# Even groups across batch borders, two shared PSUM banks for small products, a table that sets the order, and the first batch's keys turned on TensorE

## The chip, the cores and the metric

The kernel runs on one core of one Trainium2 chip. The metric is the device time of one execution in microseconds; the number reported is the median over the executions. A core has five engines, each of which runs its own instructions strictly in its own order and waits on the others through semaphores: TensorE (matrix products and the loading of their weights), VectorE, ScalarE, GpSimd, and SyncE, whose queue only issues DMA transfers here. Products land in PSUM, eight banks of 2 KB per partition.

## The reference

Agent attention is followed by a maxout feed-forward network of three branches. There are B = 4 batches of N = 12544 tokens with C = 128 channels, 49 agents per batch, and a hidden width of 768:

```python
scale = 1.0 / np.sqrt(q.shape[-1])
def sm(a, b):
    s = scale * (a @ b.transpose(0, 2, 1))
    s = s - s.max(-1, keepdims=True)
    e = np.exp(s)
    return e / (e.sum(-1, keepdims=True) + 1e-09)
agent_v = sm(agents, k) @ v          # agents look at all keys of their batch
x = sm(q, agents) @ agent_v          # each token looks at the 49 agents
h = np.maximum(np.maximum(x @ w1, x @ w2), x @ w3)
out = h @ w_out                      # 50176 x 128, float32
```

The inputs q, k, v and the result are 25.7 MB each in float32. All keys and values of a batch must be seen before the first token of that batch can be finished.

## The kernel before

**Tiles and groups.** A batch is 98 tiles of 128 tokens. Tiles go in groups of eight (GT = 8), so a batch has 12 full groups and one of two tiles: 13 groups, 52 in all (NG = 13). Each group exists twice, as a key group (`k_group`) and as a query group (`q_group`).

**Key group.** k and v are loaded (512 KB each), cast to bf16 on GpSimd (for batch 0 the v cast is on ScalarE), and k is turned by a DMA transpose (L159). TensorE makes the scores of 49 agents for each tile (L166), ScalarE the exponentials (`e_k`, L171), TensorE the weighted sums of v and the sums of the exponentials (`values`, L178 and L180, 16 small products), and VectorE adds them to `Eacc` (L189).

**Tail of a batch's keys.** `k_tail` divides (L208 to L211) and multiplies the result by the combined weights `wall`, in four products of 512 or 256 columns (L220) whose copies alternate between ScalarE (L225) and VectorE (L223). This gives G, the 49 x 1792 matrix with which a query's exponentials are turned straight into hidden units. The weights are stored as differences (w2 - w1, w3 - w1), so that the maximum of three becomes relu, add, maximum, and what is left is linear in x.

**Query group.** Eight tiles are loaded, cast and turned by DMA (L253). The scores with the agents (L259) go through the exponential on ScalarE (`e_q`, L264). For each of six hidden chunks f there is a first pair of products into a tile of two PSUM banks (`uv_ps`, L287, called u below), a relu on ScalarE into `a_sb` (L301), a second pair (v, L287) and the maximum with `a_sb` on VectorE into r (L312). For the last chunk, f = 5, ScalarE applies relu in place (L298), the second pair adds on top, and ScalarE's relu (L310) writes r5. The two products of a pair use partitions 0-48 and 64-112. The output comes in two halves o = 0, 1 of four tiles: two linear products (L317), then 24 products with `wo_bf` (L326), and a scale by `recips` on VectorE (L333). The row sums for `recips` come from four tiny products (L273), which share a PSUM tile with the key scores of the same moment, and a reciprocal (L279). One store (L340) writes the group.

**PSUM.** `uv` has three tiles of two banks; "o" (an output half) has one bank, and "m" (scores, sums, key values, k_tail's products) has one.

**Order.** Each step is recorded with a number by `at(key, fn)`; at the end all steps are sorted by it and issued in that order, so the numbers set the order on every engine, SyncE's queue too. One query group takes 6 units. Loads stand 24 units ahead, casts 14, transposes 8 to 10. The keys of batch b run beside the queries of batch b - 1, a group ahead, so the last batch's queries run with no keys beside them, and batch 0's keys run alone at the start.

## Time and profile before

| what | us |
|---|---|
| median of 3 runs | 605.72 (605.44 to 606.43) |
| the profiled execution | 602.93 |
| its span, first to last instruction | 601.1 |
| TensorE busy | 471.4 (78%) |
| VectorE busy | 383.8 (64%) |
| ScalarE busy | 412.5 (69%) |
| GpSimd busy | 140.3 (23%) |

Busy times come from the first part of the profile's page. Matrix products overlap and their ends are modelled in the profile, so TensorE's share is no share of its peak. An instruction's row names its line in the kernel, the engine, the operation, the output and inputs by tile name, shapes and a count; the idle time of the engine just before stands in brackets with what ended it. The mean granted clock of TensorE is 0.948 of full speed.

### The profile page before, as it was taken

To read this page: it belongs to the slowest core of one execution; us is meant where nothing else is said; L and a number is where in the kernel's file an instruction comes from. 1 tells how busy PE (TensorE), PEld (TensorE's weight loads), DVE (VectorE), ACT (ScalarE), POOL (GpSimd) and SP (SyncE) were. 2 spreads that over 40 slices of the span, in tenths; PEclk is the share of its full clock that TensorE was granted. 3 is DMA by queue.
4 is the path that set the end of the run, shared out by engine and by line. 5 is a ranking of instruction groups with operands and counts; after the bars stand their busy time and mean duration, and the time that the engine had idled before them with its cause. 6 is when DMAs were issued, how large, how long until landed. Compare 5 with 4: busy or idle time off the path is not lost.

```text
span 601.1 us, 13157 instructions
## 1 busy us (share of the span) xinstructions
PE 471.4 (78%) x5320; PEld 285.2 (47%) x5320; DVE 383.8 (64%) x499; ACT 412.5 (69%) x493; POOL 140.3 (23%) x149
## 2 busy tenths in 40 slices
PE   0343588898987889888887878889896898889886
PEld 0333245555553545555553545555553444545454
DVE  1200267878786556878776568787875667766774
ACT  2542378787875667787875678878784577777773
POOL 1223543233142232323142232322000101010000
PEclk9999999999998969999997989999996889988999
DMA  8999999999898797989986899995732625533222
GB/s 325 370 340 343 341 275 303 270 294 219 252 239 225 222 277 198 270 269 202 255 261 196 216 284 224 284 257 159 181 110 53 189 77 147 145 119 101 67 75 81
DMA packets 135112, 130.99 MB, mean 218 GB/s; under 512 B 107079, under 2 KB 110091, under 8 KB 135051
## 3 DMA queue, kind: packets, MB, share of 16 engines
q1 hardware_dynamic: 133632, 128.48, 76.7%
q10 hardware_dynamic: 1419, 1.67, 0.8%
q8 instruction: 41, 0.67, 0.5%
q14 instruction: 20, 0.16, 0.1%
HBM read 78.74 MB, written 25.69 MB: 174 GB/s over the span
## 4 chain that ended last, share of the span: by engine, by line
PE 49%; ACT 18%; DVE 15%; DMA 9%; issue 6%; SPq 1%; POOL 1%; ACTq 0%; POOLq 0%; DVEq 0%
PE uv_ps L287 20%; PE o_ps L326 18%; ACT a_sb L301 14%; DVE r L312 12%; DMA kT<-k_bf 6%; PE o_ps L317 4%; PE m_ps L259 3%; DVE o_sb L333 3%; ACT r L310 2%; DMA qT<-q_bf 1%; PE m_ps L178 1%; PE m_ps L180 1%; DMA wst<-in_moe_w_dram 1%; PE m_ps L220 1%; POOL k_bf L150 1%
## 5 line engine op out<-in xcount | busy, mean ns | idle before, releaser
L312 DVE TENSOR_TENSOR r<-uv_ps,a_sb 128x1024 bf16<-128x1024 f32 (+1 forms) x260 | 295.0, 1158 | 40.7 <-ACT a_sb L301 27.7
L301 ACT ACTIVATE a_sb<-uv_ps 128x1024 bf16<-128x1024 f32 (+1 forms) x260 | 248.3, 975 | 71.7 <-PE uv_ps L287 69.9
L287 PE MATMUL uv_ps<-e_q,G 49*128 49x512 bf16 (+1 forms) x1248 | 211.8, 391 | 55.0 <-ACT a_sb L301 43.6
L326 PE MATMUL o_ps<-wo_bf,r 128*128 128x128 bf16 x2352 | 184.1, 227 | 0.0
L326 PEld LDWEIGHTS <-r 128*128 128x128 bf16 x2352 | 144.4, 101 | 52.0 <-issue 49.2
L287 PEld LDWEIGHTS <-G 49*128 49x128 bf16 x1248 | 65.5, 95 | 131.8 <-issue 93.4
L333 DVE TENSOR_TENSOR o_sb<-o_ps,recips 128x512 f32<-128x512 f32 (+1 forms) x100 | 67.0, 670 | 95.1 <-PE o_ps L326 95.1
L249 POOL CAST q_bf<-q_st 128x1024 bf16<-128x1024 f32 (+1 forms) x52 | 51.7, 994 | 154.3 <-DMA qT<-q_bf 150.0
L155 POOL CAST v_bf<-v_st 128x1024 bf16<-128x1024 f32 (+1 forms) x39 | 38.7, 993 | 207.4 <-PE m_ps L180 187.2
L298 ACT ACTIVATE uv_ps<-uv_ps 128x1024 f32<-128x1024 f32 (+1 forms) x52 | 49.9, 959 | 28.5 <-DVE r L312 16.0
L310 ACT ACTIVATE r<-uv_ps 128x1024 bf16<-128x1024 f32 (+1 forms) x52 | 50.7, 975 | 21.5 <-PE uv_ps L287 21.4
L150 POOL CAST k_bf<-k_st 128x1024 bf16<-128x1024 f32 (+1 forms) x52 | 51.9, 998 | 55.5 <-DMA kT<-k_bf 46.4
L317 PE MATMUL o_ps<-G,e_q 128*128 128x256 bf16 x196 | 40.3, 287 | 12.7 <-DVE o_sb L333 12.5
L166 PE MATMUL m_ps<-agT,kT 128*128 128x49 bf16 x392 | 20.9, 196 | 25.7 <-DMA kT<-k_bf 24.4
L178 PE MATMUL m_ps<-e_k,v_bf 128*128 128x49 bf16 x392 | 30.8, 195 | 8.7 <-ACT e_k L171 8.7
L171 ACT ACTIVATE e_k<-m_ps 128x392 bf16<-128x392 f32 (+1 forms) x52 | 25.0, 480 | 16.1 <-PE m_ps L166 15.8
L189 DVE TENSOR_TENSOR Eacc<-m_ps,Eacc 128x98 f32<-128x98 f32 x48 | 10.6, 221 | 35.7 <-PE m_ps L180 35.7
L264 ACT ACTIVATE e_q<-m_ps 128x512 bf16<-128x512 f32 (+1 forms) x52 | 29.5, 568 | 3.7 <-PE m_ps L259 3.6
L317 PEld LDWEIGHTS <-e_q 128*128 128x128 bf16 x196 | 15.0, 98 | 35.1 <-issue 34.5
L180 PE MATMUL m_ps<-e_k,ones 128*128 128x49 bf16 x392 | 30.9, 194 | 0.0
L180 PEld LDWEIGHTS <-ones 128*128 128x128 bf16 x392 | 26.0, 103 | 10.0 <-issue 10.0
L166 PEld LDWEIGHTS <-kT 128*128 128x128 bf16 x392 | 17.3, 104 | 28.3 <-DMA kT<-k_bf 25.7
(43 smaller groups left out, 137.3 us busy)
## 6 DMA issues: line engine op xcount, KB each, us to landing
k_st<-in_k_dram SPq DMA_DIRECT2D x48, 512.0 KB, 5.4
v_st<-in_v_dram SPq DMA_DIRECT2D x48, 512.0 KB, 6.2
q_st<-in_q_dram SPq DMA_DIRECT2D x48, 512.0 KB, 4.2
out_dram<-o_sb SPq DMA_DIRECT2D x48, 512.0 KB, 2.9
wst<-in_moe_w_dram ACTq DMA_DIRECT2D x3, 384.0 KB, 7.8
kT<-k_bf SPq DMA_TRANSPOSE x52, 5.2
qT<-q_bf SPq DMA_TRANSPOSE x52, 4.5
k_st<-in_k_dram SPq DMA_DIRECT2D x4, 128.0 KB, 4.6
```

The costliest lines, as they stand in the source:

```text
L150: nc.gpsimd.tensor_copy(out=d["kb"][:, :n, :], in_=d["k"][:, :n, :])
L155: nc.gpsimd.tensor_copy(out=d["vb"][:, :n, :], in_=d["v"][:, :n, :])
L180: nc.tensor.matmul(t[:, c + A:c + 2 * A], ones, e, start=False, stop=True, skip_group_check=True)
L249: nc.gpsimd.tensor_copy(out=d["qb"][:, :n, :], in_=d["q"][:, :n, :])
L287: nc.tensor.matmul(t[:, h, :T], G[b][h * H:h * H + A, col + f * P:col + (f + 1) * P], d["e"][h * H:h * H + A, :T], start=start, stop=True, ...
L298: nc.scalar.activation(u, u, AF.Relu)
L301: nc.scalar.activation(a_sb[f][:, :, :T], u, AF.Relu)
L310: nc.scalar.activation(r[:, :, :T], u, AF.Relu)
L312: nc.vector.tensor_tensor(out=r[:, :, :T], in0=u, in1=a_sb[f][:, :, :T], op=ALU.max)
L317: nc.tensor.matmul(t[:, i * 2 * C:(i + 1) * 2 * C], d["e"][:, jj * P:(jj + 1) * P], G[b][:, C1O:C1O + 2 * C], start=(i == 0), stop=False, ...
L326: nc.tensor.matmul(t[:, c:c + C], r_sb[f][:, h, jj * P:(jj + 1) * P], wo_bf[:, f, :], start=False, stop=(f == NF - 1), skip_group_check=True)
L333: nc.vector.tensor_tensor(out=d["out"][:, j:j + m, :], in0=d["o", o][:, :m * C].rearrange("p (j c) -> p j c", c=C), in1=d["r"][:, j:j + m] ...
```

## The change

The two files differ in five ways.

1. **Even groups.** The tiles of all batches are one row of 392, cut into 49 groups of eight. Three query groups and the key groups at the borders hold tiles of two batches (`split`); their scores, hidden products, loads and stores are issued in one piece per batch. Batch 0's keys keep 12 groups and one of two tiles, and one key group of six tiles completes the cut.
2. **Small PSUM tiles.** "o" and "m" become one pool of two banks ("om"), which output halves, scores, sums and key products take in turn. k_tail's products (now two, of 1024 and 768 columns, one copied by ScalarE and one by VectorE), and the weight preparation, take `uv` tiles.
3. **Order.** A table `KEY` gives every step of a group its own number. Output products are issued per hidden chunk (`oc01`: half 0, chunk 1), four at a time.
4. **First batch's keys.** They are turned by eight TensorE transposes into a `uv` tile and a VectorE copy (`evacuate`) in place of the DMA transpose.
5. **Buffers.** Loads get four buffers in place of three, the casts of k and q three in place of two, that of v four.

On VectorE, in a regular group with keys beside it, before and after (r0 to r5 are the maxima of hidden chunks, `recips` the reciprocal, `o_sb` an output half's scale, `Eacc` the keys' accumulation):

```order
L312 TENSOR_TENSOR r1_4444<-uv_ps_4428,a_sb_4417 128x1024
L312 TENSOR_TENSOR r2_4484<-uv_ps_4450,a_sb_4446 128x1024
L279 RECIPROCAL recips_4486<-m_ps_4419 128x8
L189 TENSOR_TENSOR Eacc_2820<-m_ps_4419,Eacc_2820 128x98
L333 TENSOR_TENSOR o_sb_4491<-o_ps_4403,recips_4315 128x512
L312 TENSOR_TENSOR r3_4499<-uv_ps_4493,a_sb_4488 128x1024
L312 TENSOR_TENSOR r4_4535<-uv_ps_4505,a_sb_4501 128x1024
L333 TENSOR_TENSOR o_sb_4491<-o_ps_4517,recips_4315 128x512
L312 TENSOR_TENSOR r0_4586<-uv_ps_4561,a_sb_4559 128x1024
```

```order
L371 TENSOR_TENSOR r0_4449<-uv_ps_4437,a_sb_4431 128x1024
L371 TENSOR_TENSOR r1_4484<-uv_ps_4472,a_sb_4440 128x1024
L340 RECIPROCAL recips_4492<-m_ps_4451 128x8
L392 TENSOR_TENSOR o_sb_4519<-o_ps_4397,recips_4321 128x512
L224 TENSOR_TENSOR Eacc_2760<-m_ps_4451,Eacc_2760 128x98
L371 TENSOR_TENSOR r2_4534<-uv_ps_4516,a_sb_4460 128x1024
L371 TENSOR_TENSOR r3_4575<-uv_ps_4544,a_sb_4490 128x1024
L371 TENSOR_TENSOR r4_4595<-uv_ps_4549,a_sb_4498 128x1024
L392 TENSOR_TENSOR o_sb_4519<-o_ps_4531,recips_4321 128x512
L371 TENSOR_TENSOR r0_4620<-uv_ps_4608,a_sb_4602 128x1024
```

The reciprocal and the accumulation stood behind r2, now the reciprocal stands behind r1, and the scale of the first output half between it and the accumulation.

On TensorE, around the key values of such a group, before and after (`v_bf` and `ones` are the weights of the key values, `uv_ps` the hidden products, `m_ps` scores, `o_ps` an output half):

```order
L326 MATMUL o_ps_6412<-wo_bf_91,r5_6399 128x128
L178 LDWEIGHTS v_bf_6012
L178 MATMUL m_ps_6428<-e_k_6451,v_bf_6012 128x49
...
L180 MATMUL m_ps_6428<-e_k_6451,ones_72 128x49
L287 LDWEIGHTS G_4820
L287 MATMUL uv_ps_6502<-e_q_6380,G_4820 128x512
...
L287 MATMUL uv_ps_6505<-e_q_6380,G_4820 128x512
...
L287 MATMUL uv_ps_6514<-e_q_6380,G_4820 128x512
...
L287 MATMUL uv_ps_6523<-e_q_6380,G_4820 128x512
...
L317 MATMUL o_ps_6526<-G_4820,e_q_6209 128x256
...
L259 MATMUL m_ps_6529<-qT_6290,agT_74 64x512
```

```order
L385 MATMUL o_ps_4397<-wo_bf_91,r4_4424 128x128
L214 LDWEIGHTS v_bf_4069
L214 MATMUL m_ps_4451<-e_k_4470,v_bf_4069 128x49
...
L217 MATMUL m_ps_4451<-e_k_4470,ones_72 128x49
L346 LDWEIGHTS G_2826
L346 MATMUL uv_ps_4516<-e_q_4391,G_2826 128x512
...
L346 MATMUL uv_ps_4522<-e_q_4391,G_2826 128x512
...
L319 MATMUL m_ps_4527<-qT_4311,agT_74 64x512
...
L376 MATMUL o_ps_4531<-G_2826,e_q_4219 128x256
```

Four hidden pairs followed the key values, and the linear products stood ahead of the next query scores; now two hidden pairs follow, then the query scores, then the linear products of the second half.

In SyncE's queue, where the first query group's transpose is issued, before and after:

```order
L159 DMA_TRANSPOSE kT_576<-k_bf_538 128x2x128
L245 DMA q_st_582<-in_q_dram 128x1024
L144 DMA k_st_584<-in_k_dram 128x1024
L144 DMA v_st_586<-in_v_dram 128x1024
L159 DMA_TRANSPOSE kT_616<-k_bf_578 128x8x128
L245 DMA q_st_624<-in_q_dram 128x1024
L144 DMA k_st_626<-in_k_dram 128x1024
L144 DMA v_st_628<-in_v_dram 128x1024
L253 DMA_TRANSPOSE qT_635<-q_bf_618 128x8x128
```

```order
L167 DMA k_st_624<-in_k_dram 128x768
L167 DMA v_st_626<-in_v_dram 128x768
L305 DMA q_st_661<-in_q_dram 128x1024
L167 DMA k_st_667<-in_k_dram 128x1024
L167 DMA v_st_669<-in_v_dram 128x1024
L305 DMA q_st_700<-in_q_dram 128x1024
L167 DMA k_st_706<-in_k_dram 128x1024
L167 DMA v_st_708<-in_v_dram 128x1024
L188 DMA_TRANSPOSE kT_734<-k_bf_702 128x6x128
L305 DMA q_st_736<-in_q_dram 128x1024
L167 DMA k_st_742<-in_k_dram 128x1024
L167 DMA v_st_744<-in_v_dram 128x1024
L313 DMA_TRANSPOSE qT_746<-q_bf_732 128x8x128
```

Before, transposes of keys stand between the loads; now the batch's key loads are all issued, and the first DMA transpose is that of the six-tile key group, ahead of the first query transpose.

The diff, without what only follows from the new index names:

```diff
+    NK = -(-NT // GT)
+    NQ = B * NT // GT
...
+    KEY = {
+        "s": -0.90, "ex": -0.41, "u0": 0.94, "u1": 0.95, "a0": 1.77, "v0": 2.04, "a1": 2.06,
...
-    def uv_tile():
-        return psum.tile([P, 2, 512], FP32, tag="uv", bufs=3, name="uv_ps")
-
-    def o_tile():
-        return psum.tile([P, 512], FP32, tag="o", bufs=1, name="o_ps")
-
-    def m_tile(dtype=FP32):
-        return psum.tile([P, 512 if dtype == FP32 else 1024], dtype, tag="m", bufs=1, name="m_ps")
+    def uv_tile(dtype=FP32):
+        return psum.tile([P, 2, 512 if dtype == FP32 else 1024], dtype, tag="uv", bufs=3, name="uv_ps")
+
+    def small_tile(name, dtype=FP32):
+        return psum.tile([P, 512 if dtype == FP32 else 1024], dtype, tag="om", bufs=2, name=name)
...
+
+    def prep_linear():
+        t = uv_tile(BF16)
...
+    def split(t0, t1, step):
+
+        parts = []
+        for t in range(t0, t1, step):
+            i = (t - t0) // step
+            if parts and parts[-1][0] == t // NT:
+                parts[-1][2] = i + 1
+            else:
+                parts.append([t // NT, i, i + 1])
+        return parts
...
         def transposes():
             d["kT"] = work.tile([P, GT, P], BF16, tag="kT", bufs=3, name="kT")
-            nc.sync.dma_start_transpose(out=d["kT"][:, :n, :],
-                                        in_=d["kb"][:, :n, :].rearrange("p j c -> p (j c)"))
+            if early:
+                t = d["kT_ps"] = uv_tile(BF16)
+                for j in range(n):
+                    nc.tensor.transpose(t[:, 0, j * P:(j + 1) * P], d["kb"][:, j, :], ident)
+            else:
+                nc.sync.dma_start_transpose(out=d["kT"][:, :n, :],
+                                            in_=d["kb"][:, :n, :].rearrange("p j c -> p (j c)"))
+
+        def evacuate():
+            nc.vector.tensor_copy(out=d["kT"][:, :n, :].rearrange("p j c -> p (j c)"),
+                                  in_=d["kT_ps"][:, 0, :n * P])
...
+        cols = {b: 0 if i else GT * A for i, (b, _, _) in enumerate(parts)}
+
         def values():
             t = d["s"]
-            c = GT * A
-            for j in range(n):
+            for j in reversed(range(n)):
                 e = d["e"][:, j * A:(j + 1) * A]
-                nc.tensor.matmul(t[:, c:c + A], d["vb"][:, j, :], e, start=False, stop=True,
+                c = cols[batch[j]]
+                nc.tensor.matmul(t[:, c:c + A], d["vb"][:, j, :], e,
+                                 start=(len(parts) > 1 and j == n - 1), stop=True,
...
+        if early:
+            at(key - 24, load)
+            at(key - 5, cast)
+            at(key, transposes)
+            at(key + 0.5, evacuate)
+            at(key + 6.6, scores)
+            at(key + 7, exps)
+            at(key + 13.2, values)
+            at(key + 13.6, accumulate)
+        else:
+            at(key - 22, load)
+            at(key - 11, cast)
+            at(key - 6.5, transposes)
+            at(key + KEY["ks"], scores)
+            at(key + KEY["ke"], exps)
+            at(key + KEY["kv"], values)
+            at(key + KEY["ka"], accumulate)
...
-        def product(i):
-            c0, c1 = i * 512, min((i + 1) * 512, WC)
-            t = m_tile()
-            for h in range(2):
-
-                c = c0 + (C if c0 >= C1O and h == 0 else 0)
...
+        def product(c0, c1, on_vector):
+            t = uv_tile()
+            cuts = [c for c in range(c0, c1, 512)] + [c1]
+            for i, (a, z) in enumerate(zip(cuts, cuts[1:])):
+                for lo, hi in ((a, min(z, C1O)), (max(a, C1O), z)):
...
+                        c = lo + (C if lo >= C1O and h == 0 else 0)
+                        nc.tensor.matmul(t[h * H:(h + 1) * H, i, lo - a:hi - a], d["avT"],
+                                         wall[:, c:c + hi - lo], start=True, stop=True,
+                                         skip_group_check=True)
+            src = t.rearrange("p i c -> p (i c)")[:, :c1 - c0]
+            if on_vector:
+                nc.vector.tensor_copy(out=G[b][:, c0:c1], in_=src)
+            else:
+                nc.scalar.activation(G[b][:, c0:c1], src, AF.Copy)
 
         at(key, normalise)
-        for i in range(-(-WC // 512)):
-            at(key + 0.02 * (i + 1), lambda i=i: product(i))
...
         def hidden(f, col, start):
-            if start:
-                t = uv_tile()
-            else:
-                t = uv[f]
-            for h in range(2):
-                nc.tensor.matmul(t[:, h, :T], G[b][h * H:h * H + A, col + f * P:col + (f + 1) * P],
-                                 d["e"][h * H:h * H + A, :T], start=start, stop=True,
-                                 skip_group_check=True)
+            t = uv_tile() if start else uv[f]
+            for b, j0, j1 in parts:
+                for h in range(2):
+                    nc.tensor.matmul(t[:, h, j0 * P:j1 * P],
+                                     G[b][h * H:h * H + A, col + f * P:col + (f + 1) * P],
+                                     d["e"][h * H:h * H + A, j0 * P:j1 * P], start=start and j0 == 0,
+                                     stop=True, skip_group_check=True)
             return t
...
-        def out_hidden(o, part):
+        def out_hidden(o, f):
             t = d["o", o]
-            for i, h, f in part:
-                jj = pairs[o][i]
-                c = (i * 2 + h) * C
-                nc.tensor.matmul(t[:, c:c + C], r_sb[f][:, h, jj * P:(jj + 1) * P], wo_bf[:, f, :],
-                                 start=False, stop=(f == NF - 1), skip_group_check=True)
+            for i, jj in enumerate(pairs[o]):
+                for h in range(2):
+                    c = (i * 2 + h) * C
+                    nc.tensor.matmul(t[:, c:c + C], r_sb[f][:, h, jj * P:(jj + 1) * P], wo_bf[:, f, :],
+                                     start=False, stop=True, skip_group_check=True)
...
+        cut = 6.0 * (s + 1) + KEY["u0"] - 0.2 if s + 1 in tails else 1e9
         at(key - 24, load)
-        at(key - 14, cast)
-        at(key - 10.2, transposes)
+        at(key - 13, cast)
+        at(key - 9, transposes)
+        at(key + KEY["s"], scores)
+        at(key + KEY["ex"], exps)
+        at(key + KEY["sum"], sums)
+        at(key + KEY["rec"], recips)
         for f in range(NF):
-            at(key + f - 0.95, lambda f=f: first(f))
-            at(key + f - 0.4, lambda f=f: relu_first(f))
-            at(key + f, lambda f=f: second(f))
-            at(key + f + 0.5, lambda f=f: max_second(f))
-        e = key + 6
...
-            at(e + linear, lambda o=o: out_linear(o))
-            for i in range(parts):
-                part = whole[i * per:(i + 1) * per]
-                at(e + first_step + i, lambda o=o, part=part: out_hidden(o, part))
-            at(e + scaled, lambda o=o: out_scale(o))
+            for name, fn in (("u", first), ("a", relu_first), ("v", second), ("x", max_second)):
+                at(min(key + KEY[f"{name}{f}"], cut), lambda f=f, fn=fn: fn(f))
+        for o in range(2):
+            at(key + KEY[f"lin{o}"], lambda o=o: out_linear(o))
+            for f in range(NF):
+                at(key + KEY[f"oc{o}{f}"], lambda o=o, f=f: out_hidden(o, f))
+            at(key + KEY[f"sc{o}"], lambda o=o: out_scale(o))
+        at(key + KEY["sc1"] + 1.5, store)
...
+    first_key = -6.0 * (NK + 2) - 4
+    at(first_key - 30, prep)
+    at(first_key + 24, prep_weights)
+    at(first_key + 36, prep_linear)
+    for g in range(NK):
+        k_group(g * GT, min((g + 1) * GT, NT), first_key + 6.0 * g, True)
+    k_tail(0, first_key + 6.0 * NK + 8)
+    if NT % GT:
+        k_group(NT, NK * GT, -6.0, False)
+    for i in range(NK, NQ):
+        k_group(i * GT, (i + 1) * GT, 6.0 * (i - NK), False)
+    tails = {b * NT // GT: b for b in range(1, B)}
+    for s, b in tails.items():
+        k_tail(b, 6.0 * s + KEY["u0"] - 0.15)
+    for s in range(NQ):
+        q_group(s)
```

163 lines of the change are left out of this document (71 added, 92 removed), and 7 rows, old and new, of the table KEY.

## The prediction

> **What bounds the kernel now.** I read the busy time by stage first, then single regular groups, then the order on the engines. The columns of a window are its length, busy time and count for TensorE, its weight loads, VectorE, ScalarE and GpSimd, the granted clock, the DMA share and GB/s:
>
> ```profile
> 0.00:72.00 72.00, 23.28 (x348) 17.38 (x350) 10.83 (x34) 24.52 (x34) 23.23 (x29) 1.00 1.07 345
> 72.00:450.14 378.14, 323.25 (x3790) 197.31 (x3786) 272.04 (x341) 286.54 (x341) 106.23 (x110) 0.95 0.89 238
> ```
>
> The first 72 us hold no output work: TensorE is busy for 23 of them. Then two regular groups, one with the key stage of the next batch beside it, one after all keys are done:
>
> ```profile
> 257.55:267.29 9.74, 8.48 (x108) 5.37 (x108) 7.54 (x9) 7.88 (x10) 3.01 (x3) 1.00 0.88 262
> 498.33:507.76 9.43, 8.23 (x84) 4.64 (x82) 7.21 (x9) 7.44 (x9) 1.16 (x2) 1.00 0.48 141
> ```
>
> A group takes 9.74 us with keys and 9.43 us without. ScalarE fills 7.88 and 7.44 of them, VectorE 7.54 and 7.21, and DMA moves 262 GB/s. So no engine but TensorE (8.48 and 8.23) is near full, and the profile models the ends of its products. The chain that ended last says the same:
>
> ```profile
> PE 49%; ACT 18%; DVE 15%; DMA 9%; issue 6%; SPq 1%; POOL 1%; ACTq 0%; POOLq 0%; DVEq 0%
> ```
>
> TensorE's order, broken by two waits per group, sets the period. Here are its bursts in that group (start, duration, count, idle before):
>
> ```profile
> 257.55 0.61 PE L287 MATMUL uv_ps<-e_q,G 49*128 49x512 bf16 x4
> 258.40 0.38 PE L317 MATMUL o_ps<-G,e_q 128*128 128x256 bf16 x2 [0.24 <-DVE o_sb L333]
> 258.62 0.61 PE L326 MATMUL o_ps<-wo_bf,r 128*128 128x128 bf16 x8
> 259.06 0.36 PE L166 MATMUL m_ps<-agT,kT 128*128 128x49 bf16 x8
> 259.36 0.61 PE L287 MATMUL uv_ps<-e_q,G 49*128 49x512 bf16 x4
> 259.90 0.62 PE L326 MATMUL o_ps<-wo_bf,r 128*128 128x128 bf16 x8
> 260.45 0.39 PE L287 MATMUL uv_ps<-e_q,G 49*128 49x512 bf16 x2
> 260.77 0.25 PE L273 MATMUL m_ps<-sel,e_q 128*128 128x2 bf16 x4
> 261.14 0.39 PE L287 MATMUL uv_ps<-e_q,G 49*128 49x512 bf16 x2
> ...
> 261.92 0.19 PE L178 MATMUL m_ps<-e_k,v_bf 128*128 128x49 bf16 x1
> ...
> 262.43 0.82 PE L287 MATMUL uv_ps<-e_q,G 49*128 49x512 bf16 x6
> 264.15 0.39 PE L287 MATMUL uv_ps<-e_q,G 49*128 49x512 bf16 x2 [0.90 <-ACT a_sb L301]
> ```
>
> I take a burst's price from start to next start. Hidden products (L287) run in pairs: four cost 0.54, two 0.32, six about 0.76, and of each about 0.1 is the turn to another kind of product. Eight output products (L326) cost 0.44, or 0.55 when a hidden burst follows; two linear ones (L317) 0.22; key scores 0.30, key values 0.51, sums 0.37; query scores, also two of 512 columns, I take as 0.33. At 257.55 four hidden products should leave 0.85 after 0.43 but wait for the single "o" bank, and at 262.43 six are followed only after 1.72 instead of 0.65. These two waits are 0.42 + 1.07 = 1.49 us; without them the sequence is 9.74 - 1.49 = 8.25.
>
> **The regular group after the change.** The new order has 6 hidden bursts per group (4, 2, 2, 6, 4, 6) where 7 stood, and the same products. Its bursts in order, at the prices above: 0.54 (u0, u1), 0.77 (outputs x12), 0.32 (v0), 0.33 (outputs x4), 0.32 (u2), 0.30 (key scores), 0.22 (x4), 0.37 (sums), 0.76 (v1, u3, u4), 0.45 (x8), 0.51 (key values), 0.54 (v2, u5), 0.33 (query scores), 0.77 (linear, x8), 0.76 (v3, v5, v4), 0.44 (x8), 0.55 (linear, x4) = 8.28 us. So the work for TensorE stays; what can be won is the 1.49 of waits, if the new order has fewer. For that I lay ScalarE and VectorE beside it:
>
> ```profile
> 247.95 1.93 ACT L301 ACTIVATE a_sb<-uv_ps 128x1024 bf16<-128x1024 f32 x2
> ...
> 255.81 0.59 ACT L264 ACTIVATE e_q<-m_ps 128x512 bf16<-128x512 f32 x1
> ```
>
> ```profile
> 252.80 0.21 DVE L279 RECIPROCAL recips<-m_ps 128x8 f32<-128x8 f32 x1 [0.16 <-PE m_ps L180]
> ...
> 253.05 0.68 DVE L333 TENSOR_TENSOR o_sb<-o_ps,recips 128x512 f32<-128x512 f32 x1
> 253.65 2.35 DVE L312 TENSOR_TENSOR r<-uv_ps,a_sb 128x1024 bf16<-128x1024 f32 x2
> ```
>
> ScalarE starts a second relu 0.91 after a first, with the result at 1.02; e_q takes 0.59. VectorE starts a second maximum 1.13 after a first (2.35 for two, result at 1.2), reciprocal and accumulation follow at 0.12 each, and out_scale holds it for 0.60. A burst of two is ready for its reader 0.43 after its start (the 0.39 of the row and a hand-over of 0.04). With u0 at 0: relu a0 0.43-1.45, a1 to 2.36, a2 2.39-3.41, e_k to 3.8, a3 3.82-4.84, a4 to 5.75. VectorE finishes the last group's scale at 1.88, r0 at 2.99, and v1 stands at 3.17, so r1 runs 3.60-4.80. Here is the one wait I find: the recips row now stands behind r1, and the key values on TensorE wait for recips, since they share one tile. At 0.06 per hand-over that lets the values start at 5.1 and not at 4.4. Behind them in TensorE's queue stand v2, u5, the next query scores and the second output half; all shift by 0.7. Then v2 at 5.6, u5 ready at 6.25, its relu to 7.25, query scores at 6.15 (their bank was freed by out_scale at 5.6), v3, v5, v4 from 7.25 (the second of them needs the relu at 7.25 and comes at 7.47), e_q to 7.75, r5 7.9-8.9, and the next u0, which needs r5's bank, at 9.0. So **9.0 us with keys**: 8.28 plus 0.7. Without keys neither scores nor values nor that wait are there (8.28 - 0.70 = 7.58); u3, u4, u5 and the query scores then wait 0.1 to 0.3 each for relus and scale, and the layout closes at **8.1**. Bounds: from below 8.3 and 7.6 (no wait at all), from above 9.74 and 9.43 (every old wait finds a new place). I take the layout's, since each of its steps has a row.
>
> The second small bank costs nothing: it takes the "o" wait of 0.42 away and is the same space as before. In the K stage DMA must carry 2.6 MB per group (three loads, one store of 0.52, two transposes of 0.26), 290 GB/s at 9.0 us; the start ran at 345 with a share of 1.07, so I count no wait, and see the rivals.
>
> **Borders.** The same relu (of a regular place in the order) around the three borders, start and duration in us:
>
> ```profile
> 177.14 1.03 ACT a_sb L301
> ...
> 311.74 1.03 ACT a_sb L301
> ...
> 443.48 1.03 ACT a_sb L301
> ...
> 488.90 1.03 ACT a_sb L301
> ```
>
> Twelve full groups and a small one lie between the first two: 134.60 - 12 x 9.74 = 17.7 for a border with its small group. The next is 131.74 - 116.9 = 14.9, the last (three groups at 9.43) 45.42 - 28.3 = 17.1. Together 49.7 us. The new kernel has 49 even groups in place of 52, so the small ones (2 of 8 tiles, at nearly half a group's instructions) are gone, and the tail that builds G is two products and two copies in a row of three 2-bank tiles instead of four, each waiting for the single bank:
>
> ```profile
> 185.71 0.18 PE L180 MATMUL m_ps<-e_k,ones 128*128 128x49 bf16 x1
> 187.17 0.41 PE L220 MATMUL m_ps<-wall,avT 128*64 128x512 bf16 x2 [1.27 <-DVE avT L211]
> 188.26 0.41 PE L220 MATMUL m_ps<-wall,avT 128*64 128x512 bf16 x2 [0.69 <-ACT G L225]
> ...
> 190.90 1.46 PE L287 MATMUL uv_ps<-e_q,G 49*128 49x512 bf16 x6
> ```
>
> The normalise chain is 1.3 and each product step 1.1-1.2. New: normalise stands behind r3 and r4 on VectorE (done at 9.9 in the layout), takes 0.75, first product 0.65, copy 1.0 on ScalarE; then u0, due at 9.0, starts at 12.4: 3.4 late. A group of two batches has its hidden products cut in two, 12 more pairs at about 0.05: 0.6. And the clock falls here:
>
> ```profile
> 189.00:192.00 3.00, 1.86 (x10) 0.67 (x10) 1.40 (x4) 0.62 (x2) 1.04 (x1) 0.65 1.03 393
> 192.00:195.00 3.00, 2.31 (x15) 0.98 (x13) 2.29 (x3) 2.19 (x3) 0.00 (x0) 0.50 0.22 87
> ```
>
> At half clock TensorE's bursts take longer; two windows of 3 us passed below full clock. I add 2 us, and take **6 per border, 18 in all** (bounds 4, with the clock up, and 9, twice such a fall). The clock staying up gives 516 - 6 = 510, and I hold it for 0.1 of the chances, inside the forecast's 0.55. The Trainium skill, "TensorE: Matmul & The Clock Gate", section "HAM oscillation", asks for no idle gap over about 3.4 us. By that rule gaps of 1.7 and 1.1 us would leave the clock alone, which is the 510. The trace disagrees: gaps of 1.27 and 0.69 ended in 0.65 and 0.50.
>
> **The start.** Of 13 early groups, keys are turned by eight transposes and a copy from a uv bank in place of a DMA transpose. Two pure-load stretches and the weights' queue:
>
> ```profile
> 5.00:8.00 3.00, 0.35 (x4) 0.21 (x4) 1.50 (x5) 1.06 (x1) 0.77 (x1) 1.00 1.01 401
> 8.00:12.00 4.00, 0.00 (x0) 0.00 (x0) 0.00 (x0) 0.25 (x1) 1.04 (x1) 1.00 1.04 402
> ```
>
> ```profile
> q10 hardware_dynamic: 1419, 1.67, 0.8%
> ```
>
> The keys and values of a batch are 12.85 MB and the weights 1.67: 14.5 MB at 402 GB/s is 36 us, from 2 us on: 38, where the loads before took turns with 13 transposes. Cast (1.0), turn and copy (1.7), scores, exps, values (2), an estimate from like operations of the same sizes, end at about 44. But q's first DMA transpose stands in SP's queue behind the loads of three more key groups and three q groups, 5.5 MB or 14 us. Before it took this long to land, and the first relu of the first and of the third group ran here:
>
> ```profile
> 61.99 8.09 DMA qT<-q_bf
> ...
> 72.09 1.03 ACT a_sb L301
> ```
>
> ```profile
> 93.78 1.03 ACT a_sb L301
> ```
>
> Landing was 8.09 after issue, and 2 us later the first relu ran. Now issue at about 45.5 plus 8.1, or 38 + 14 + 1: both give 53-54, and the first relu at **56** in place of 72.1. Bounds: 49, if q is ready when G is; 72, if the start is bound by something the trace does not show. Casts (ScalarE 1.06 + 0.50 per group) fit in the 2.8 us that a group's load takes. The Trainium skill, "DMA: Bandwidth & Descriptors", section "Where 436 GB/s comes from", gives about 358 GB/s for a core's loads from HBM; by it they end 4 us later (sum 520, inside the forecast). The rows of 401 and 402 disagree.
>
> **The end.** In the last group r4 is done 8.6 after the first relu, then come 0.22 of products, scale 0.7, the second half's products 1.7, scale 0.7, and the store:
>
> ```profile
> out_dram<-o_sb SPq DMA_DIRECT2D x48, 512.0 KB, 2.9
> ```
>
> With 2.9 for landing, about 14.5 from the first relu of the last group.
>
> **Sum.** 56 + 2.2 (the first two groups took 93.78 - 72.09 = 21.7 in place of 2 x 9.74) + 36 x 9.0 = 324 + 18 + 12 x 8.1 = 97.2 + 14.5 = 511.9 us of span. The profiled execution took 602.93 for a span of 601.1, 1.83 more, and the median of the runs shown is 605.72, 2.79 above that. So 511.9 + 4.6 = **516 us**.
>
> **Rivals.** (1) The order wins nothing in a regular group, because each wait only moves; start and borders are still won. For it: every hidden product still waits for one of three 2-bank tiles. Against it: the old 0.90 wait came from two tiles asked for in a row, which the new order spreads. 516 + 36 x 0.73 + 12 x 1.33 = 558. (2) No wait at values, and q early: 8.4 and 7.9, start 49: 516 - 21.6 - 2.4 - 7 = 485. For it: VectorE has 1.5 us to spare per group. (3) DMA decides in the 36 groups with keys: transposes come late since 290 GB/s with stores is more than the 262 of a regular group. Were it held to 262, a group takes 10.0: 516 + 36 = 552. Against it: 345-402 in the start. (4) Slower: one small bank carries key scores, e_k, recips, values, accumulation, then an output half until its scale, and only then the next key scores. The bare steps are 0.5 + 0.5 + 0.2 + 0.6 + 0.2 + 0.2 + 1.5 + 0.7 = 4.4 us. If each of its three steps on VectorE sits behind two maxima (2 x 1.2 x 3 = 7.2), the loop is 11.6 and 49 groups take 49 x 2.6 = 127 more: 644. It decides above 9.0 and makes the kernel slower above 10.8 (605.7 - 516 over 49 groups). Against it: in VectorE's new order at most one maximum stands right ahead of each.
>
> **Chances.** Forecast 0.55 (its own range 498-534: +-0.3 per group, the start 50-60, borders 4-9), (1) 0.15, (2) 0.16, (3) 0.10, (4) 0.03, no difference 0.01. Leaving out most of (4) and the ends of (1) and (2), 8 in 10 lie in 484-556. Changes under 0.2%, 1.2 us, cannot be told from none here: faster 0.96, same 0.01, slower 0.03.
>
> **What would show it.** Regular groups of 9.0 and 8.1 between like relus; TensorE's longest wait per group under 0.8 and before the key values, released by recips; the first relu near 56 after a q transpose that lands late; key-transposes gone from SP's queue before 45; at each border a wait of 1.7 before G's products and a clock below 1. Wrong, if a regular group still takes over 9.4 or the relu's gap (1.0 and more) moves to a DMA transpose; if loads in the start stay at 345 GB/s; or if the clock falls inside regular groups.

## The result, and the profile after

| | us |
|---|---|
| before, median of the runs beside it | 605.58 (603.61 to 606.43) |
| after, median | 514.49 (512.98 to 516.38) |
| ratio | 0.8501 (95% interval 0.8466 to 0.8536) |
| predicted | 516, range 484 to 556 |
| the profiled execution of after, and its span | 512.98, 511.0 |

The total is 1.5 us from the forecast, but its terms are not all so close: errors of up to 10 us cancel, and that they do is luck. The page of after, first the busy times, then the chain that ended last:

```profile
PE 450.0 (88%) x5426; PEld 277.5 (54%) x5426; DVE 391.5 (77%) x488; ACT 404.4 (79%) x463; POOL 141.3 (28%) x142
...
DMA 47%; PE 22%; SPq 14%; POOL 8%; DVE 4%; issue 3%; ACT 1%; ACTq 0%; POOLq 0%; DVEq 0%
```

TensorE is busy for 88% of the span (78% before). The chain is now 47% DMA and 14% issues by SyncE (SPq), where before TensorE had 49% and DMA 9%. One regular group with keys and one without, from one `e_q` to the next (columns as in the prediction):

```profile
206.19:214.90 8.71, 8.34 (x108) 5.15 (x106) 7.58 (x10) 7.82 (x10) 2.60 (x3) 1.00 1.03 297
412.64:420.69 8.05, 7.99 (x84) 4.47 (x82) 7.28 (x8) 7.44 (x10) 1.04 (x1) 1.00 0.56 166
```

A group takes 8.71 and 8.05 us in place of 9.74 and 9.43. With keys DMA now has a share of 1.03 at 297 GB/s. TensorE's one wait, and VectorE beside it:

```profile
210.89 0.97 PE L346 MATMUL uv_ps<-e_q,G 49*128 49x512 bf16 x6
211.79 0.62 PE L385 MATMUL o_ps<-wo_bf,r 128*128 128x128 bf16 x8
212.78 0.18 PE L214 MATMUL m_ps<-e_k,v_bf 128*128 128x49 bf16 x1 [0.37 <-DVE recips L340]
...
213.28 0.60 PE L346 MATMUL uv_ps<-e_q,G 49*128 49x512 bf16 x4
213.81 0.41 PE L319 MATMUL m_ps<-qT,agT 128*64 128x512 bf16 x2
```

```profile
211.39 1.22 DVE L371 TENSOR_TENSOR r<-uv_ps,a_sb 128x1024 bf16<-128x1024 f32 x1 [0.36 <-PE uv_ps L346]
212.53 0.20 DVE L340 RECIPROCAL recips<-m_ps 128x8 f32<-128x8 f32 x1
212.65 0.64 DVE L392 TENSOR_TENSOR o_sb<-o_ps,recips 128x512 f32<-128x512 f32 x1
```

TensorE stands idle for 0.37 ahead of the key values until `recips`, which runs behind r1, is done: the wait that the prediction named (0.7 there). The rest of the group is TensorE's bursts back to back. Not foreseen are two groups in the second batch, here by ScalarE's `e_q`, TensorE's wait, and SyncE's issues:

```profile
249.77 0.59 ACT L325 ACTIVATE e_q<-m_ps 128x512 bf16<-128x512 f32 x1
...
261.01 0.60 ACT L325 ACTIVATE e_q<-m_ps 128x512 bf16<-128x512 f32 x1 [2.10 <-PE m_ps L319]
...
272.70 0.59 ACT L325 ACTIVATE e_q<-m_ps 128x512 bf16<-128x512 f32 x1
```

```profile
260.34 0.64 PE L319 MATMUL m_ps<-qT,agT 128*64 128x512 bf16 x2 [2.53 <-DMA qT<-q_bf]
```

```profile
250.46 4.58 SPq L313 DMA_TRANSPOSE qT<-q_bf  x1
255.13 3.99 SPq L188 DMA_TRANSPOSE kT<-k_bf  x1
```

Two intervals are 11.24 and 11.69 in place of 8.72: q's transpose came 2.53 late, and behind the gap the clock was at 0.50 to 0.65 for 6 us:

```profile
258.00:261.00 3.00, 0.66 (x3) 0.23 (x4) 0.86 (x1) 0.92 (x1) 0.00 (x0) 0.71 0.79 158
261.00:264.00 3.00, 3.00 (x20) 1.57 (x21) 0.98 (x1) 1.16 (x2) 0.66 (x1) 0.50 0.95 330
264.00:267.00 3.00, 3.00 (x29) 2.00 (x27) 1.40 (x3) 1.29 (x2) 1.42 (x2) 0.65 0.91 314
```

SyncE's issue of a q transpose takes 4.58 here and that of the keys 3.99 us. The medians are 1.71 and 3.99 in after, 1.47 and 1.49 before (from the view of each tile). The first border:

```profile
168.29 0.39 PE L385 MATMUL o_ps<-wo_bf,r 128*128 128x128 bf16 x4
170.43 1.66 PE L269 MATMUL uv_ps<-wall,avT 128*64 128x512 bf16 x10 [1.75 <-DVE avT L257]
172.03 0.29 PE L346 MATMUL uv_ps<-e_q,G 49*128 49x128 bf16 x2
172.57 0.93 PE L346 MATMUL uv_ps<-e_q,G 49*128 49x384 bf16 x6 [0.26 <-ACT G L276]
```

```profile
168.00:171.00 3.00, 1.25 (x15) 0.81 (x14) 2.34 (x5) 0.59 (x1) 1.78 (x2) 0.92 1.30 339
171.00:174.00 3.00, 2.75 (x25) 1.33 (x20) 0.96 (x1) 1.91 (x2) 0.30 (x1) 0.51 1.00 133
174.00:177.00 3.00, 3.00 (x51) 1.91 (x49) 2.33 (x3) 2.54 (x5) 0.23 (x1) 1.00 1.01 316
```

The wait for the normalise chain is 1.75 (1.7 in the prediction), and the clock falls to 0.51 after it. At the second border the wait is 1.75 again and the clock falls to 0.50. At the third it is 1.75 too, but the clock stays at 1.00:

```profile
396.61 0.95 PE L269 MATMUL uv_ps<-wall,avT 128*64 128x512 bf16 x10 [1.75 <-DVE avT L257]
```

```profile
397.00:400.00 3.00, 2.47 (x37) 1.40 (x32) 1.56 (x2) 2.39 (x3) 0.00 (x0) 1.00 0.03 5
```

The start, on TensorE (G's products, the scores of the first key group beside queries, the first query scores), and the first relu:

```profile
49.52 1.71 PE L269 MATMUL uv_ps<-wall,avT 128*64 128x512 bf16 x10 [1.50 <-DVE avT L257]
54.11 0.43 PE L199 MATMUL m_ps<-agT,kT 128*128 128x49 bf16 x6 [2.89 <-DMA kT<-k_bf]
...
58.94 0.64 PE L319 MATMUL m_ps<-qT,agT 128*64 128x512 bf16 x2 [3.18 <-DMA qT<-q_bf]
```

```profile
60.92 1.94 ACT L361 ACTIVATE a_sb<-uv_ps 128x1024 bf16<-128x1024 f32 x2 [0.70 <-PE uv_ps L346]
```

### The profile page after: what moved, and what is told of

The parts are those of the page before. It is cut to its first block, busy times and chain, and to the rows that moved or that the text cites. A ratio compares the mean times of both kernels' runs of the same rounds, so it can differ in the third digit from the quotient of the medians.

```text
span 511.0 us, 13285 instructions
## 1 busy us (share of the span) xinstructions
PE 450.0 (88%) x5426; PEld 277.5 (54%) x5426; DVE 391.5 (77%) x488; ACT 404.4 (79%) x463; POOL 141.3 (28%) x142
## 4 chain that ended last, share of the span: by engine, by line
DMA 47%; PE 22%; SPq 14%; POOL 8%; DVE 4%; issue 3%; ACT 1%; ACTq 0%; POOLq 0%; DVEq 0%
DMA v_st<-in_v_dram 25%; DMA k_st<-in_k_dram 16%; PE uv_ps L346 9%; PE o_ps L385 9%; SPq L188 7%; SPq L305 4%; POOL v_bf L179 4%; DVE r L371 3%; POOL k_bf L174 3%; DMA q_st<-in_q_dram 3%; SPq L167 3%; DMA wst<-in_moe_w_dram 2%; PE o_ps L376 2%; DMA kT<-k_bf 1%; PE m_ps L319 1%
## 5 line engine op out<-in xcount | busy, mean ns | idle before, releaser
L371 DVE TENSOR_TENSOR r<-uv_ps,a_sb 128x1024 bf16<-128x1024 f32 x245 | 295.2, 1222 | 54.6 <-PE uv_ps L346 46.5
L361 ACT ACTIVATE a_sb<-uv_ps 128x1024 bf16<-128x1024 f32 x245 | 244.8, 1024 | 32.0 <-PE uv_ps L346 28.3
L346 PE MATMUL uv_ps<-e_q,G 49*128 49x512 bf16 (+3 forms) x1248 | 198.0, 383 | 4.2 <-ACT G L276 1.4
L309 POOL CAST q_bf<-q_st 128x1024 bf16<-128x1024 f32 x49 | 51.0, 1042 | 242.0 <-DMA q_st<-in_q_dram 241.8
L392 DVE TENSOR_TENSOR o_sb<-o_ps,recips 128x512 f32<-128x512 f32 x98 | 66.0, 674 | 14.4 <-PE o_ps L385 10.7
L174 POOL CAST k_bf<-k_st 128x1024 bf16<-128x1024 f32 (+2 forms) x50 | 51.2, 1025 | 53.5 <-DMA k_st<-in_k_dram 48.1
L358 ACT ACTIVATE uv_ps<-uv_ps 128x1024 f32<-128x1024 f32 x49 | 49.5, 1011 | 11.5 <-PE uv_ps L346 11.0
L369 ACT ACTIVATE r<-uv_ps 128x1024 bf16<-128x1024 f32 x49 | 50.2, 1024 | 8.3 <-PE uv_ps L346 3.8
L179 POOL CAST v_bf<-v_st 128x1024 bf16<-128x1024 f32 (+1 forms) x37 | 38.3, 1036 | 26.5 <-DMA v_st<-in_v_dram 16.5
L325 ACT ACTIVATE e_q<-m_ps 128x512 bf16<-128x512 f32 x49 | 29.0, 592 | 6.7 <-PE m_ps L319 6.7
L214 PEld LDWEIGHTS <-v_bf 128*128 128x128 bf16 x392 | 27.3, 103 | 0.5 <-issue 0.5
```

The lines of the kernel that those rows point to most:

```text
L174: nc.gpsimd.tensor_copy(out=d["kb"][:, :n, :], in_=d["k"][:, :n, :])
L179: nc.gpsimd.tensor_copy(out=d["vb"][:, :n, :], in_=d["v"][:, :n, :])
L214: nc.tensor.matmul(t[:, c:c + A], d["vb"][:, j, :], e, start=(len(parts) > 1 and j == n - 1), stop=True, skip_group_check=True)
L309: nc.gpsimd.tensor_copy(out=d["qb"], in_=d["q"])
L346: nc.tensor.matmul(t[:, h, j0 * P:j1 * P], G[b][h * H:h * H + A, col + f * P:col + (f + 1) * P], d["e"][h * H:h * H + A, j0 * P:j1 * P], s ...
L358: nc.scalar.activation(u, u, AF.Relu)
```

## The experiments

Two theories are held against each other below. **A:** in the stage with keys DMA is at its limit, and an engine that gets faster only meets late transposes in more places. **B:** the order on the engines sets the length of this stage, as the prediction had it. A covers two things that the runs below do not separate: the transfers themselves, and SyncE's queue, which issues them one after another. The stage's length is counted from the `e_q` of query group 1 to that of group 36, 35 groups and two borders. In after:

```profile
68.30:393.02 324.72, 305.11 (x3766) 186.62 (x3765) 268.23 (x324) 276.07 (x318) 104.19 (x100) 0.95 1.06 273
```

324.72 us are 9.28 a group: 35 x 8.715 = 305.0, 10.9 more at two borders, 5.5 in the two groups above, 2.5 in group 1 at half clock, and some tenths. The DMA share is 1.06 on the mean, at 273 GB/s.

**1. The first batch's keys by DMA again.**

```diff
-            at(key - 5, cast)
-            at(key, transposes)          # eight TensorE transposes
-            at(key + 0.5, evacuate)
+            at(key - 8, cast)
+            at(key - 2.2, transposes)    # nc.sync.dma_start_transpose
```

> The changed kernel with one part undone: the first batch's keys are turned by DMA transposes again (cast 3 units earlier, transpose 2.2 units ahead of the old TensorE turn, no copy from PSUM). Theory: the start is set by the stream of loads, and transposes in it slow the stream, so the first relu goes from 60.9 us back toward the 72.1 of the kernel before; everything behind is shifted whole, so 514.5 + 8 to 12 = 522 to 527. Rival: the start came from the deeper load buffers and the new weight order, and the turning on TensorE is worth nothing: first relu within 2 us of 60.9, time within 2 us of 514.5.

530.04 us, ratio 0.8773 (0.8722 to 0.8825): 15.5 more than after, above the range expected. The first relu (ScalarE's row in this run):

```profile
76.22 2.85 ACT L351 ACTIVATE a_sb<-uv_ps 128x1024 bf16<-128x1024 f32 x3 [0.70 <-PE uv_ps L336]
```

76.22 against 60.92. Each of SyncE's transposes stands ahead of later loads and takes 1.2 to 3.1 us to issue, so the last load of this batch ends its issue at 47.07 in place of 35.41 (SyncE's rows of both). The turning on TensorE is worth 15 us, more than the start gained against before (72.09).

**2. The old order** in the new structure (table filled with the old numbers, output products in 3 + 2 pieces).

> The changed kernel with the old order: the table holds the numbers of the kernel before, and output products are issued in three and two pieces as there; the even groups, the shared pair of small banks (which with these numbers alternate just as the two single banks did), the buffers, the k_tail in two products and the first batch's keys on TensorE stay. Theory: the two TensorE waits per group (0.42 and 1.07 us) come back and a group takes 9.74 us with keys and 9.43 without, in place of 8.72 and 8.05: 514.5 + 36 x 1.02 + 12 x 1.38 = 568. Rival, the banks and buffers alone give the gain of a group: within 5 us of 514.5. Rival between, the 0.42 wait stays away: 568 - 48 x 0.42 = 548.

551.86 us, ratio 0.9123 (0.9081 to 0.9164). This lies between the theory's 568 and the 548 of the rival between, nearer to the latter. An undisturbed group takes 9.64 with keys and 9.43 without (`e_q` to `e_q`). The one regular wait left on TensorE is the old one:

```profile
236.10 0.39 PE L342 MATMUL uv_ps<-e_q,G 49*128 49x512 bf16 x2 [0.90 <-ACT a_sb L357]
```

The 0.42 wait on the "o" bank is gone with the second bank: the linear products at 230.15 start before the scale of the half ahead of them ends at 230.40, so the two stand in different banks. Yet the period falls by 0.10 only: the burst of four hidden products that follows takes 0.83 in place of 0.54. So the order gives 0.92 x 36 + 1.38 x 12 = 50 us, and 37 arrive. The rest is lost in the two slow groups of after (5.5; this run waits for no q transpose but the first) and at the borders, which cost 2.0 to 2.3 us over a group here and 3.5 to 6.4 in after, since the old numbers put normalise earlier.

**3. The reciprocal ahead of the second maximum.**

```diff
-        "rec": 3.76
+        "rec": 3.05
```

> The changed kernel with one number moved: the reciprocal of the row sums stands ahead of the second maximum on VectorE, not behind it, so the key values on TensorE no longer wait for it. Theory (the order of TensorE's bursts and its waits set the period): the wait of 0.38 us ahead of the values goes and a group with keys takes 8.72 - 0.38 = 8.35 us; 514.5 - 36 x 0.37 = 501. Rival 1, DMA (share 106% of its queue in this stage) sets the period: groups stay at 8.7 and the time within 2 us of 514.5. Rival 2, the wait moves to the maxima, each 0.2 us later: a gain under 5 us.

512.06 us, ratio 0.8486 (0.8433 to 0.8538), where 501 was forecast: no difference from after that can be told. A group takes 8.78, not 8.35. VectorE:

```profile
224.57 0.21 DVE L340 RECIPROCAL recips<-m_ps 128x8 f32<-128x8 f32 x1 [0.80 <-ACT e_k L204]
224.70 1.17 DVE L371 TENSOR_TENSOR r<-uv_ps,a_sb 128x1024 bf16<-128x1024 f32 x1
```

`recips` and the keys' exponentials read one tile, and the reciprocal, recorded behind them, waits for them: 0.80 us, in which r1 cannot start. The wait moved, much as the second rival had it; the run says nothing yet on A and B.

**4. The same with the reciprocal ahead of the exponentials too** (`"rec": 2.70`, in front of `"ke": 2.78`).

> The changed kernel with the reciprocal recorded ahead of the keys' exponentials (2.70 in the table in place of 3.76), so that it neither stands behind the second maximum nor waits for the exponentials as it did in the run with 3.05 (0.80 us). The wait of 0.37 ahead of the key values should go, and an undisturbed group with keys take 8.35 to 8.4 us by any theory. Theory A (DMA sets the length of the stage): more groups are disturbed by late query transposes, the 35 groups still average about 9.2, and the time is 509 to 515. Theory B (engines): 514.5 - 36 x 0.35 = 502.

509.69 us, ratio 0.8432 (0.8371 to 0.8494). A regular group and the stage:

```profile
198.47:206.71 8.24, 8.24 (x108) 5.02 (x106) 7.49 (x9) 7.73 (x11) 2.77 (x3) 1.00 0.99 270
66.90:388.14 321.24, 301.58 (x3770) 183.14 (x3768) 266.38 (x324) 273.81 (x319) 104.04 (x100) 0.96 1.05 277
```

```profile
PE m_ps L319 <- DMA qT<-q_bf: 17.1, 12, 3.2
```

The group is 8.24 with TensorE busy for all of it: the prediction's sum of bursts was 8.28. But 35 groups take 321.24, only 3.5 less than in after where 35 x 0.47 = 16.5 were to be won. TensorE waits 12 times for q's transposes, 17.1 us in all (after: 3 times, 6.0), at places spread over the stage. This speaks for A. (The intervals of this run and of after overlap, so the 4.8 us themselves are not clear of noise.) One other reason for late transposes can be looked up: a store in SyncE's queue waits for its scale on VectorE, and everything behind it waits too. In this stage these waits come to 8.5 us (32.6 in after), so they are not what makes more transposes late here.

**5. and 6. Without the stores of the first 36 groups,** with the reciprocal as in after, and moved:

```diff
-        at(key + KEY["sc1"] + 1.5, store)
+        if s >= 36:
+            at(key + KEY["sc1"] + 1.5, store)
```

> The changed kernel without the stores of the first 36 query groups (left out: most of the result is not written), one sixth to one fifth of the bytes of the stage with keys. No engine's order changes but SyncE's. Theory A: the late query transposes vanish, all groups but the borders take 8.72, and the 5.5 us of the two slow groups and some at the second border go: 503 to 508. Theory B: late transposes are a matter of their place in SyncE's queue alone, and the time is within 3 us of 514.5.

> Both at once: the reciprocal ahead of the exponentials, and no stores of the first 36 query groups (most of the result is left out). Theory A: with DMA below its limit the 0.35 us per group now count: 36 x 0.35 = 12.6 less than without stores alone, 491 to 495, while the same move with the stores in place was worth at most 5. Theory B: the move is worth the same 12 us with and without stores, 502 both times.

505.14 us, ratio 0.8355 (0.8307 to 0.8403), and 487.21, ratio 0.8035 (0.7981 to 0.8090). The first lies in A's range, the second below it. Without stores, the reciprocal's move is worth 18 us by the medians (12.5 between the spans of the two profiled executions; that of the second run is its longest, 491.14), with them 4.8. The waits for q's transposes of the two runs:

```profile
PE m_ps L319 <- DMA qT<-q_bf: 3.2, 1, 3.2
```

```profile
PE m_ps L319 <- DMA qT<-q_bf: 3.5, 2, 3.2
```

One wait and two are left, of which 3.2 is the start's. The keys' transposes issue in 1.61 us (median) in the first of the two, 3.99 in after. What makes an issue long is not settled. In after, each transpose of keys follows that of q at once, with loads issued just ahead of both. In run 8, where the order of the two is turned round, q's is the long one (median 3.90, the keys' 2.25). In before they follow each other at once too and stay short, but there SyncE had stood idle for 4.6 us behind the last load (243.81 to 248.44):

```profile
248.89 1.46 SPq L253 DMA_TRANSPOSE qT<-q_bf  x1
250.46 1.46 SPq L159 DMA_TRANSPOSE kT<-k_bf  x1
```

So a long issue goes with many transfers put into the queue at once, not with the rate alone: run 2 moves 258 GB/s in its stage and has a median of 3.68, the group of before 262 GB/s and 1.49. These issues nearly fill SyncE's queue. Its rows add up to 270 us of issues in the 324.7 of after's stage, 294 in the 321.2 of run 4 and 309 in the 328.7 of run 8. In the first run without stores it is 177 in 314.9. The stores are also 36 issues fewer (0.38 each), so the transfers' limit and that of the queue cannot be told apart; issuing the stores from another engine's queue would separate them, and no run does it.

**7. Normalise early at the borders.**

```diff
-        at(key, normalise)
+        at(key - 2.07, normalise)
```

> The changed kernel with one step moved: at the three borders the division that makes the agents' values (normalise) stands right behind the last accumulation of the batch's keys on VectorE, not behind two more maxima; the products and copies stay where they were. Theory A (DMA sets the length of the stage with keys: its share is over 1.0 from 60 to 372 us, 35 groups take 9.28 on average though an undisturbed one takes 8.72): the wait of 1.75 ahead of G's products goes, but the transposes for the next queries then come late by as much, and the time is within 3 us of 514.5. Theory B (the engines' order sets it): 3 x 1.75 = 5 us less, and up to 8 if the clock no longer falls: 506 to 509.

511.17 us, ratio 0.8450 (0.8410 to 0.8490). The first border:

```profile
166.58 0.95 PE L269 MATMUL uv_ps<-wall,avT 128*64 128x512 bf16 x10
167.58 0.23 PE L346 MATMUL uv_ps<-e_q,G 49*128 49x128 bf16 x2
168.32 0.55 PE L346 MATMUL uv_ps<-e_q,G 49*128 49x384 bf16 x6 [0.51 <-ACT G L276]
```

```profile
165.50:168.50 3.00, 2.44 (x32) 1.64 (x31) 2.96 (x3) 1.92 (x2) 1.04 (x1) 1.00 1.00 304
168.50:171.50 3.00, 3.00 (x54) 2.10 (x51) 1.88 (x3) 2.76 (x3) 2.08 (x2) 1.00 1.11 282
171.50:174.50 3.00, 2.63 (x45) 1.55 (x41) 2.65 (x5) 2.74 (x5) 0.00 (x0) 1.00 1.13 273
```

The 1.75 wait is gone and the clock stays at 1.00. The three borders cost 2.0, 2.7 and 1.9 us over a group (4.5, 6.4 and 3.5 in after): 7.8 us won there, of which 3.3 show, and the third border's 1.6 is behind the stage. These are single executions, and a border varies between them: the first costs 3.5 in run 5 and 6.8 in run 6. The stage itself takes 324.8 us, as in after (324.7), with 10 waits for q's transposes, 13.0 us. A again.

**8. Query casts and transposes three units earlier.**

> The changed kernel with the casts of q 16 units ahead in place of 13 and its DMA transposes 12 ahead in place of 9. Theory: the two late transposes (groups of 11.24 and 11.69 us in place of 8.72) and the late ones of the first groups are a matter of lead alone, so about 5.5 us go and perhaps 2 at the start: 507 to 509. Rival: DMA is full in this stretch, and an earlier transpose takes its place from a load that GpSimd then waits for (it waits 11 us for q loads already): stalls appear elsewhere, and the time is 512 to 520.

510.58 us, ratio 0.8464 (0.8419 to 0.8510): between the two ranges expected, and not to be told from after. The first relu comes at 57.27 and TensorE waits for no q transpose at all. But the stage takes 328.7, and the waits are now for the keys' transposes, which stand behind q's in the queue (in after one such wait, 2.9):

```profile
PE m_ps L199 <- DMA kT<-k_bf: 10.7, 8, 3.5
```

Lead for the one moved the stall to the other. A again.

**9. The first query group early.**

```diff
-    k_group(NT, NK * GT, -6.0, False)
+    k_group(NT, NK * GT, -6.0, False, (30, 14.5, 11))   # load, cast, turn ahead of key; were 22, 11, 6.5
...
+        lead = 1.0 if s else 0.0
-        at(key - 24, load)
+        at(key - 24 * lead - 46 * (1 - lead), load)   # and the cast at 27, the transpose at 23
```

> The changed kernel with the first query group's load, cast and transpose moved ahead in their queues (22, 14 and 14 units), and those of the first key group that runs beside queries (8, 3.5, 4.5 units); nothing else. Step of the prediction under test: the first relu is late because q's transpose stands behind the loads of other groups. If so, the first relu moves from 60.9 to 54 to 57. Theory A then gives 2 to 4 us of that back in more late transposes: 510 to 514. Theory B gives all of it: 508 to 510.

515.36 us, ratio 0.8519 (0.8482 to 0.8557), above both ranges. SyncE at the start:

```profile
38.76 0.33 SPq L167 DMA_DIRECT2D v_st<-in_v_dram  x1
45.72 1.34 SPq L313 DMA_TRANSPOSE qT<-q_bf  x1
47.13 0.56 SPq L167 DMA_DIRECT2D k_st<-in_k_dram  x1
```

The first relu moves from 60.92 to 58.91 only, not to 54 to 57, and the second group's `e_q` comes 11.8 behind the first's (8.7 in after). Moved ahead of the loads, the transpose makes SyncE wait for the cast from 39.1 to 45.7 while no load is issued. What the first group gains, the second gives back.

**10. Twelve stores kept back** until the last batch's queries, with the reciprocal of 4.

```diff
+    LATE = [2 + 3 * i for i in range(12)]
...
+                wait = s in LATE
+                d["out"] = work.tile([P, GT, C], FP32, tag="o_late" if wait else "o_sb",
+                                     bufs=len(LATE) if wait else 3, name="o_sb")
...
-        at(key + KEY["sc1"] + 1.5, store)
+        at(6.0 * (NQ - 12) + 4.0 * LATE.index(s) if s in LATE else key + KEY["sc1"] + 1.5, store)
```

> The reciprocal ahead of the exponentials, and 12 of the stores of the stage with keys (of query groups 2, 5, ... 35) kept in 12 buffers of their own and issued beside the last batch's queries, where DMA is half idle; the whole result is written. Theory A (DMA sets the length of the stage): a store of 0.52 MB at some 280 GB/s is 1.87 us of DMA, a third of them kept back takes 0.62 us off the average of 9.2 to 9.3 per group, so it falls to 8.6 to 8.7, about what the run without any stores needed: 488 to 496. Theory C, only leaving work out helps and the kept stores cost the last stage what they save: within 4 us of 509.7.

494.37 us, ratio 0.8175 (0.8139 to 0.8210), in A's range: 15 less than without keeping back, for the same work. The stage takes 305.1 us. DMA in the stage's last part and beside the last batch's queries, in after and here:

```profile
300.00:340.00 40.00, 38.13 (x491) 23.28 (x489) 34.82 (x44) 36.13 (x43) 14.91 (x15) 1.00 1.10 299
400.00:480.00 80.00, 79.05 (x834) 44.86 (x833) 72.25 (x80) 73.55 (x80) 8.34 (x8) 1.00 0.57 152
```

```profile
300.00:340.00 40.00, 40.00 (x520) 24.39 (x519) 36.24 (x45) 37.91 (x45) 14.24 (x14) 1.00 1.06 277
400.00:480.00 80.00, 79.31 (x818) 44.54 (x815) 73.55 (x80) 73.90 (x80) 6.24 (x6) 1.00 0.67 186
```

The last batch's stage takes the kept stores at a share of 0.67. The share over the whole stage is 1.06 at 273 GB/s, the same as in after, though nearly all groups now take 8.24: a share above 1 alone does not tell that groups are held up.

**11. All four edits** (4, 7, 9, 10).

> Everything that bore fruit, at once: the reciprocal ahead of the exponentials, 12 stores kept back, the early normalise at the borders and the first query group early; the whole result is written. Against the run with the reciprocal and the kept stores (say 492): the start gives up to 6, the borders up to 8 if DMA leaves room. Theory A: DMA is again at its limit with 12 stores kept, so about 4 to 6 in all: 485 to 489. Engines alone: 477 to 480.

499.14 us, ratio 0.8234 (0.8179 to 0.8290), where A expected 485 to 489: no faster than with 4 and 10 alone. TensorE waits 11 times, 15.0 us, for q's transposes; the start's stall is paid for here too.

**12. The same without 9,** and with 15 stores kept back, 7 of them in the first batch's queries (groups 1, 3, 4, 6, 7, 9, 10, 13, 15, 17, 20, 25, 28, 31, 34; the weights' staging tiles share the buffers).

> The reciprocal ahead of the exponentials, the early normalise at the borders, and 15 stores kept back, 7 of them in the first batch's queries, where the run with 12 evenly spread ones still had late transposes worth 4.6 us (the weights' staging tiles share the kept stores' buffers to make room); the first query group stays where the changed kernel has it. Theory A: against that run's 494.4 the 4.6 us of late transposes go and the borders give 2 to 8: 482 to 489. If DMA still binds after all: 491 to 495, with late transposes in the second and third batch, where the kept stores are as dense as before and the borders leave less slack. Nothing to gain at borders at all: 490.

487.14 us, ratio 0.8036 (0.7998 to 0.8074), in A's range: 27 us faster than after with all of the result written. Its borders cost 2.2, 2.4 and 2.0 over a group, the first batch has no slow group after group 1, and four slow ones (9.1, 9.0, 9.6, 10.6) come at 289 to 327 us, in the third batch, where q's transposes come late again. Four kept stores lie in that batch, as many as in the second, which has no slow group; why the third has them is not shown.

## Why the prediction was right, term by term

| term | predicted | measured in after |
|---|---|---|
| first relu | 56 | 60.92 |
| first two groups beyond regular ones | 2.2 (of 9.0) | 2.5 (of 8.72) |
| 36 groups with keys | 9.0 each | 8.72 |
| a late query transpose and its clock fall | none | 5.5 |
| three borders | 6.0 each, 18 | 4.5, 6.4, 3.5: 14.4 |
| 12 groups without keys | 8.1 each | 8.05 |
| end, from the last group's first relu | 14.5 | 15.6 |

**Regular group: right in cause, over-sized.** The term is "9.0 us with keys: 8.28 plus 0.7". The wait before the key values is there and released by `recips`, but it is 0.37, not 0.7. Counted from u0, r1 starts at 3.40 where the layout had 3.60, and the values start 1.39 behind it where it had 1.5 (TensorE's burst with u0 starts at 207.99; r1 and the values stand above at 211.39 and 212.78). A group is 8.72 and not 9.0, which over 36 groups makes 10 us. That TensorE's bursts are the floor is shown by run 4: 8.24 with TensorE full, against 8.28 summed. That the order removed the relu's wait is shown by run 2, where it stands again and a group takes 0.92 more with keys and 1.38 more without. Without keys the layout's 8.1 held, but the bare sum beside it, 7.58, takes off 0.70 for scores and values that it prices at 0.30 and 0.51; it should be 7.47.

**"So I count no wait" for DMA: wrong.** The step set 290 GB/s against 345 in the start. But that start has loads and one transpose per group and no stores, and the stage with keys has stores and two transposes per group. There after moves 273 GB/s at a share of 1.06, and the stage stays near 9.28 us a group on the mean with every order that is as fast as after's or faster: 321 to 330 us in after and in runs 1, 3, 4, 7, 8 and 9, 302 to 315 in runs 5, 6, 10, 11 and 12, when stores leave it. (Run 2, whose order is slower, takes 344.) Whether the transfers or SyncE's issues of them are at the limit stays open, as said at runs 5 and 6. One of the prediction's own signs of being wrong came true here: the clock fell inside regular groups, to 0.50 to 0.65 behind the late transpose. The row that told it stood in the prediction: 0.88 of 9.74 us is 8.6 us of DMA per group, hardly less than the 9.0 it forecast. Rival (3) named the mechanism and priced it at 552; the rate held was 273, not 262, and it cost 5.5 in after. That the borders' idle time let the transfers catch up is an inference from run 7, where shorter borders brought 10 late transposes in place of 3.

**Start: right on the loads, short on q.** Loads ran at 367 to 408 GB/s from 24 to 48 us. The Trainium skill, "DMA: Bandwidth & Descriptors", section "Where 436 GB/s comes from", has about 358 for HBM; the trace goes above it again. But SyncE issued no load between 12.02 and 20.18 us (294 GB/s in 16 to 24), so the last of the batch's keys and values landed at about 43.7 and not at 38, and q's transpose was issued at 49.94 where the prediction had 45.5. It landed 9.0 later (8.1 predicted). The remedy that the step suggests, q earlier in the queue, brings the first relu to 57.27 when it is moved by three units (run 8) and fails when it is moved far ahead (run 9); neither makes the whole faster beyond doubt.

**Borders: right on the wait, in part on the clock.** The wait was 1.75 against 1.7, and 14.4 us stand against 18. The clock fell at two borders of three; at the third it stayed at 1.00 behind the same wait, and that border was the cheapest (3.5). In run 7, with a gap of 0.51, it stayed at 1.00 at the first border. So a gap of 1.75 can end in half clock and need not; what decides is not shown. The Trainium skill, "TensorE: Matmul & The Clock Gate", section "HAM oscillation", asks for no idle gap over about 3.4 us, so by it the clock would have stayed up at all three; the trace of after disagrees at the first two, with 0.51 and 0.50.

**End: 15.6 against 14.5.** The parts that the step lists (8.6, 0.22, 0.7, 1.7, 0.7, 2.9) add up to 14.8.

**First bank term.** "The second small bank ... takes the 'o' wait of 0.42 away" holds, but in run 2, with the old order, it is worth 0.10 a group: the next burst of hidden products took longer in its place.
